# Square roots in batches of four chunks, paired exponentials and a new order of all queues, in a gated recurrence with a gated linear unit on one Trainium2 core

## The chip, the core and the metric

The kernel runs on one core of a Trainium2 chip. The core has a matrix engine (PE), three engines that work on whole tiles (DVE, ACT and POOL), a queue engine (SP) that here issues the transfers, and 16 DMA engines that carry them between the chip's main memory and the core's own memory, SBUF. Matrix results land in PSUM, eight banks of 128 partitions by 2 KB. Each engine works through its own list of instructions in order and waits at semaphores for the others. The metric is the device time of one execution in microseconds (us); less is better. Beside the timed runs there is one execution recorded by the hardware profiler; its span runs from the first to the last instruction.

## What is computed

The input is a batch of 4 sequences of 6336 steps with 256 channels, taken as 25344 rows. A gated linear recurrence runs along each sequence, and its result goes through a gated linear unit whose gate is a causal convolution of five taps:

```python
sig_r, sig_i = sigmoid(r_gate), sigmoid(i_gate)
a_t = np.exp(8.0 * sig_r * np.log(clip(sigmoid(a_param))))
x_gated = np.sqrt(np.maximum(1.0 - a_t * a_t, 1e-06)) * sig_i * x
for t in range(S):
    h = a_t[:, t] * h + x_gated[:, t]
    y[:, t] = h
...
gate = sigmoid(sum(conv_w[k] * shifted(y, k) for k in range(5)))
out = (gate * (y @ w_val)) @ w_out
```

So every element of the gates r and i and of x is read once, and every output is written once: about 78 MB in and 26 MB out.

## The kernel before

**Tiles.** The rows are cut into 51 windows, of 512 rows but for two of 256 at the start and one at the end, and the windows into 28 chunks (CHUNKS, line 16): the first three and the last two are small, the 23 between hold two windows, 1024 rows. Window w of a large chunk c is 2c-3 or 2c-2. Channels are handled in two halves of 128, called h.

**One chunk's way.** Loads of a window are `lr` (gate r), `li` (gate i) and `lx` (x), issued by SP. `ta` and `tb` (ACT, lines 296 and 299) take the hyperbolic tangent of r and i, from which the sigmoids follow. `tr` (PE, line 343) turns the tangent of r so that channels lie on partitions; `ex` (ACT, line 359) makes the decays a of it into `aring`. `sq` squares them into `ering` (POOL, line 367; `sa` is the same on ACT). `rt` (ACT, line 386) takes the square root over a whole batch of chunks in place. `nt` (PE, line 401) turns the roots back, and `xg` (DVE, line 408) multiplies them into `uring`, which holds the product of the input gate and x: `pp` and `up` on POOL (lines 306, 318), or, for some windows, `xp` on PE and `uv` on DVE (lines 323, 332). `xt` (PE, line 417) turns that product, and `sc` (DVE, line 439) is the recurrence itself, a scan for each half, into `yring`. For each window `cv` (PE, line 451) is the convolution, `tg` (ACT, line 458) the tangent for its sigmoid, `vl` (PE, line 466) the product with w_val, `gv` (DVE, line 471) the gating, `ou` (PE, line 481) the product with w_out, `cd` or `ca` the copy out of PSUM on DVE (line 489) or ACT (line 491), and `st` (SP, line 502) the store.

**What sets the order.** Everything stands in one string, ORDER, of words such as `tr.7.1@0,1` (operation, chunk or window, half, PSUM banks). A loop at the end emits them one by one, so that each engine's list is the string's words for that engine, in their order. [...]

**Tables.** `ta`, `tb`, `tg` and `ex` need one table of functions on ACT, `rt` another. The loop at the end keeps track and puts a table load (line 518) wherever the next word needs the other one. BATCHES (line 19) says which chunks share a root: there are ten, of three large chunks in the middle. `op_rt` emits one instruction for each stretch of the batch that is contiguous in `ering`, all at once.

**Rings.** The decays and the squares have room for 5120 columns each (NA, NE), five large chunks. A chunk's `ex` therefore overwrites the decays of the chunk five before, and has to wait until their scans are done; its `sq` overwrites squares whose roots `nt` must have read. The loads of r and of i have four window slots each, x four, the tangents of r six, of i four, the gate tile three (NTG), the output tile four.

**Groups.** GROUPS (line 32) says which chunks share one `tr` and `ex`: two neighbours in the middle, but 11, 12, 21 and 22 each alone.

ACT's list before, up to the third root and from the last but one:

```
ta.0 ta.1 ta.2 ex.0.1 ex.1.1 ex.1.0 ex.2.0 ex.0.0 ta.3 ta.4 tb.2 ex.2.1 tb.0 ex.3.1 tb.1 ex.3.0 ta.6 ta.5 tb.3
rt.0 rt.1 tb.4 ex.5.0 tg.0 tb.5 tg.1 ex.5.1 tg.2 ta.8 ta.7 tb.6 ex.7.1 ex.7.0 tb.7 tg.3 rt.2
...
rt.8 tg.41 tg.40 tb.25 ex.26.0 ca.39.0 tb.26 tg.42 ca.40.0 ex.26.1 sa.26.1 sa.26.0 ca.41.0 tg.43 tb.27 tg.44 ca.42.0
rt.9 tg.45 ca.44.0 ca.43.0 tg.46 tg.48 ca.45.0 ca.46.0 tg.47 ca.48.0 tg.49 ca.47.0 tg.50 ca.49.0 ca.50.0
```

Of the kernel before, what the change touches and what calls it, by code (L numbers as in the profile page):

```python
# [8 lines left out]
P = 128  # L9
CONV_K = 5  # L10
FP32 = mybir.dt.float32
# [7 lines left out]
BATCHES = [[0, 1, 2], [3, 4], [5, 6, 7], [8, 9, 10], [11, 12, 13], [14, 15, 16], [17, 18, 19], [20, 21, 22], [23, 24, 25],  # L19
    [26, 27]]  # L20
# [3 lines left out]
NU = 10  # L24
# [7 lines left out]
GROUPS = [[0], [1], [2], [3, 4], [5, 6], [7, 8], [9, 10], [11], [12], [13, 14], [15, 16], [17, 18], [19, 20], [21], [22],  # L32
# [3 lines left out]
s_ident s_small s_kt s_diag lr.0 ta.0 tr.0.1@0 lr.1 ta.1 lr.2 ta.2 ex.0.1 tr.1.1@1 ex.1.1 tr.1.0@2 tr.2.0@3 ex.1.0  # L36
ex.2.0 tr.0.0@0 tr.2.1@4 lr.3 lr.4 ex.0.0 sq.0.1 sq.0.0 ta.3 lr.5 lr.6 ta.4 sq.2.0 tr.3.1@0,1 li.2 lx.2 tb.2 ex.2.1
li.0 sq.1.0 s_wl.1 tb.0 lx.0 li.1 sq.1.1 ex.3.1 sq.3.1 sq.4.1 lr.7 tb.1 pp.1 tr.3.0@2,3 ex.3.0 sq.4.0 xp.0@4 uv.0 lr.9
lr.10 ta.6 xp.2@0,1 lr.8 sq.3.0 li.4 li.3 ta.5 tb.3 sq.2.1 s_wl.3 lx.1 lx.4 xp.4@2,3 lx.3 rt.0 uv.2 lx.6 li.6 s_wl.2
s_wl.0 lr.13 up.1 li.5 li.8 nt.0@0 xg.0 nt.2@1 nt.1@0 li.7 uv.4 xt.0@5,4 pp.3 up.3 lx.5 lx.7 lr.14 lr.12 rt.1 xg.1  # L40
xg.2 sc.0.1 sc.0.0 nt.3@6,7 xg.3 tb.4 li.10 lx.8 lr.11 li.9 xt.2@0,1 tr.5.0@2,3 xt.1@4,5 ex.5.0 cv.0@6,7 tg.0 sc.1.1
tb.5 li.12 sc.1.0 xt.3@5,4 sc.2.1 cv.1@6,7 tr.5.1@2,3 tg.1 ex.5.1 sc.2.0 cv.2@0,1 xp.7@6,7 sc.3.0 sc.3.1 s_wcast
vl.1@2,3 gv.1 pp.6 pp.5 vl.0@4,5 up.6 lx.10 up.5 pp.8 gv.0 nt.4@2,3 ou.0.0@4 ou.1.0@5 uv.7 tg.2 ta.8 cd.1.0 sq.6.1
lx.9 li.11 cd.0.0 st.1 st.0 ta.7 up.8 tb.6 tr.7.1@0,1 ex.7.1 xg.4 tr.7.0@6,7 ex.7.0 tb.7 lx.11 vl.2@4,5 gv.2 lr.16
lx.12 li.13 xt.4@2,3 sc.4.1 cv.3@0,1 sq.6.0 sq.5.0 sq.5.1 tg.3 vl.3@4,5 xp.9@6,7 sc.4.0 sq.7.1 sq.7.0 rt.2 lr.15 lr.18
gv.3 pp.10 sq.8.1 uv.9 vl.5@0,1 ou.3.0@4,5 ou.2.0@2,3 cd.3.0 cd.2.0 li.14 lr.17 st.3 lx.13 xp.11@6,7 cv.5@2,3 uv.11
tg.5 st.2 up.10 lx.14 li.15 li.16 pp.12 nt.5@6,7 xg.5 tb.8 li.17 up.12 lx.16 li.18 ta.10 gv.5 ta.9 lr.20 cv.6@4,5
# [502 lines left out]
```

## Time and profile before

| | |
|---|---|
| median of 3 timed runs | 294.39 us (293.57 to 295.06) |
| span of the profiled execution | 291.5 us |
| busy: ACT, DVE, PE, POOL | 275.0, 247.3, 243.8, 233.0 us |
| instructions: ACT, DVE, PE, POOL | 198, 206, 2509, 155 |
| moved by DMA | 104.75 MB, mean 359 GB/s |

The profiled execution has no time of its own beside its span; the timed runs take in what lies around the span. "Busy" counts an engine as working, not as waiting at a semaphore. Lines of groups give the source line, the engine, what is written from what with its shape, the number, the busy time, the mean of one in ns, and the idle time of the engine just before these instructions with what ended it ("<-"). Lines in order of time give the start, the duration, and the same names; instructions of one line that follow one another are merged ("x2").

### The profile page before, as it was taken

What the parts mean: (1) busy time and instruction counts of PE and PEld (TensorE: products, weight loads), DVE (VectorE), ACT (ScalarE), POOL (GpSimd) and SP (SyncE); (2) the same over time, 40 slices, a digit from 0 to 9 for tenths busy, and PEclk for the clock granted to TensorE, in tenths of its full rate; (3) what the DMA queues carried; (4) which work ended last, traced back from release to release, by engine and by line L of the source; (5) the groups of instructions that cost most, each with busy time, mean ns of one, the idle gap of its engine ahead of it and who ended that gap; (6) DMA issues with size and microseconds to landing.
All of it is one profiled execution on the core that took longest, in us unless ns stands there. A gap on an engine that the chain in (4) does not pass through costs nothing.

```text
span 291.5 us, 6283 instructions
## 1 busy us (share of the span) xinstructions
PE 243.8 (84%) x2509; PEld 167.6 (57%) x2509; DVE 247.3 (85%) x206; ACT 275.0 (94%) x198; POOL 233.0 (80%) x155
## 2 busy tenths in 40 slices
PE   2281798997986988989888988899889998999993
PEld 1141475455744766567656666657457765767662
DVE  2030589988999999999999999999999999999891
ACT  7799989999999999999999999999999999999563
POOL 1449789999899899999996599998998799976000
PEclk9996789999999999999999999999999999999999
DMA  7999999999999999999999999999999958983354
GB/s 243 356 409 388 386 408 413 338 419 414 408 417 398 388 393 400 386 347 415 412 398 384 409 410 371 411 339 386 408 414 421 413 211 322 338 329 128 147 217 181
DMA packets 29996, 104.75 MB, mean 359 GB/s; under 512 B 3335, under 2 KB 3854, under 8 KB 29966
## 3 DMA queue, kind: packets, MB, share of 16 engines
q1 hardware_dynamic: 29952, 104.35, 92.6%
q8 instruction: 19, 0.31, 0.4%
q14 instruction: 11, 0.09, 0.1%
q10 hardware_dynamic: 14, 0.01, 0.0%
HBM read 78.39 MB, written 25.95 MB: 358 GB/s over the span
## 4 chain that ended last, share of the span: by engine, by line
ACT 39%; PE 18%; DMA 17%; DVE 12%; issue 12%; SPq 1%; ACTq 0%; DVEq 0%
ACT tbring L299 9%; DMA iring<-in_i_gate_dram 8%; DMA rring<-in_r_gate_dram 8%; ACT ering L386 8%; ACT tgring L458 7%; ACT taring L296 6%; DVE yring L439 5%; PE banks L481 5%; PE banks L451 4%; ACT L518 4%; PE banks L466 3%; ACT aring L359 3%; PE banks L401 3%; DVE oring L489 2%; DVE tgring L471 2%
## 5 line engine op out<-in xcount | busy, mean ns | idle before, releaser
L367 POOL TENSOR_TENSOR ering<-aring 128x1024 f32<-128x1024 f32 (+2 forms) x54 | 91.9, 1723 | 21.4 <-ACT aring L359 21.4
L439 DVE TENSOR_TENSOR_SCAN yring<-aring,yring,banks 128x1024 bf16<-128x1024 f32 (+5 forms) x54 | 105.9, 1988 | 1.3 <-PE banks L417 1.2
L318 POOL TENSOR_TENSOR uring<-tbring,xring 128x1024 bf16<-128x1024 bf16 (+1 forms) x45 | 94.5, 2112 | 3.0 <-PE banks L481 1.3
L451 PE MATMUL banks<-yring,diag 64*64 64x512 bf16 (+7 forms) x1080 | 62.2, 361 | 3.0 <-DVE oring L489 1.7
L471 DVE SCALAR_TENSOR_TENSOR tgring<-tgring,banks 128x1024 bf16<-128x1024 bf16 (+1 forms) x51 | 59.1, 1179 | 5.3 <-PE banks L466 3.1
L466 PE MATMUL banks<-yring,wv 128*128 128x512 bf16 (+4 forms) x216 | 49.5, 361 | 8.7 <-ACT tgring L458 4.2
L359 ACT ACTIVATE aring<-banks,khf 128x2048 f32<-128x2048 bf16 (+3 forms) x38 | 54.5, 1485 | 1.1 <-PE banks L343 1.1
L458 ACT ACTIVATE tgring<-banks 128x1024 bf16<-128x1024 f32 (+1 forms) x51 | 50.5, 1014 | 5.1 <-PE banks L481 3.3
L481 PE MATMUL banks<-wo,tgring 128*128 128x256 bf16 x396 | 50.4, 274 | 5.2 <-DVE tgring L471 3.2
L306 POOL TENSOR_SCALAR tbring<-tbring 128x1024 bf16<-128x1024 bf16 (+1 forms) x45 | 45.8, 1030 | 8.3 <-ACT tbring L299 8.3
L481 PEld LDWEIGHTS <-tgring 128*128 128x128 bf16 x396 | 41.7, 114 | 14.8 <-DVE tgring L471 6.6
L296 ACT ACTIVATE taring<-rring 128x2048 bf16<-128x2048 f32 (+2 forms) x28 | 47.5, 1722 | 1.8 <-DMA rring<-in_r_gate_dram 1.8
L299 ACT ACTIVATE tbring<-iring 128x2048 bf16<-128x2048 f32 (+2 forms) x28 | 48.1, 1727 | 0.6 <-DMA iring<-in_i_gate_dram 0.6
L386 ACT ACTIVATE ering<-ering 128x2048 bf16<-128x2048 f32 (+3 forms) x13 | 44.5, 3454 | 0.1
L451 PEld LDWEIGHTS <-diag 64*64 64x64 bf16 x1080 | 29.0, 106 | 26.9 <-issue 11.4
L408 DVE TENSOR_TENSOR uring<-banks,uring 128x2048 bf16<-128x2048 bf16 (+2 forms) x28 | 30.3, 1092 | 14.7 <-PE banks L401 12.3
L489 DVE COPY oring<-banks 128x1024 f32<-128x1024 f32 (+1 forms) x35 | 40.6, 1185 | 0.8 <-PE banks L481 0.4
L343 PE MATMUL banks<-ident_b,taring 128*128 128x128 bf16 x396 | 30.2, 233 | 9.4 <-ACT taring L296 9.0
L466 PEld LDWEIGHTS <-wv 128*128 128x128 bf16 x216 | 19.7, 97 | 29.8 <-issue 14.4
L343 PEld LDWEIGHTS <-taring 128*128 128x128 bf16 x396 | 25.9, 105 | 16.1 <-ACT taring L296 11.5
L401 PE MATMUL banks<-ident,ering 128*128 128x128 f32 x198 | 29.3, 293 | 3.6 <-ACT ering L386 2.5
L401 PEld LDWEIGHTS banks<-ident,ering 128*128 128x128 f32 x198 | 26.3, 206 | 8.9 <-ACT ering L386 2.7
(37 smaller groups left out, 135.7 us busy)
## 6 DMA issues: line engine op xcount, KB each, us to landing
rring<-in_r_gate_dram SPq DMA_DIRECT2D x48, 512.0 KB, 7.5
iring<-in_i_gate_dram SPq DMA_DIRECT2D x48, 512.0 KB, 8.3
xring<-in_x_dram SPq DMA_DIRECT2D x48, 512.0 KB, 7.5
out_dram<-oring SPq DMA_DIRECT2D x48, 512.0 KB, 5.8
rring<-in_r_gate_dram SPq DMA_DIRECT2D x3, 256.0 KB, 3.0
iring<-in_i_gate_dram SPq DMA_DIRECT2D x3, 256.0 KB, 7.4
xring<-in_x_dram SPq DMA_DIRECT2D x3, 256.0 KB, 7.6
out_dram<-oring SPq DMA_DIRECT2D x3, 256.0 KB, 4.1
```

What stands on the lines that cost most here:

```text
L296: nc.scalar.activation(**tangent(c, taring, NTR, rring, NRI))
L299: nc.scalar.activation(**tangent(c, tbring, NTI, iring, NII))
L318: nc.gpsimd.tensor_tensor(out=u, in0=t1, in1=xt, op=ALU.mult)
L367: nc.gpsimd.tensor_tensor(out=e, in0=a, in1=a, op=ALU.mult)
L386: nc.scalar.activation(out=ering[:].bitcast(BF16)[:, 4 * o:4 * o + 2 * n], in_=ering[:, 2 * o:2 * o + 2 * n], func=ACT.Sqrt, scale=-0.25, ...
L401: nc.tensor.transpose(out=bank[:, k:k + P], in_=ering[:, e + q:e + wins[w] // 2:nq], identity=ident[:])
L439: nc.vector.tensor_tensor_scan(out=yring[:, h, col:col + o1 - o0], data0=aring[:, h, a_at[c] + o0:a_at[c] + o1], data1=xT[:, o0:o1], initi ...
L451: nc.tensor.matmul(out=gp[oh * 64:oh * 64 + 64, h, a:b], lhsT=diag[half * 64:half * 64 + 64, h, k, :], rhs=yring[half * 64:half * 64 + 64, ...
L458: nc.scalar.activation(out=tgring[:, w % NTG, :, 0:wins[w]], in_=live.pop(("gp", w))[:, :, 0:wins[w]], func=ACT.Tanh, scale=0.5)
L466: nc.tensor.matmul(out=val[:, m, a:b], lhsT=wv[:, hk, m * P:(m + 1) * P], rhs=yring[:, hk, col:col + b - a], start=(hk == 0), stop=(hk == ...
L471: nc.vector.scalar_tensor_tensor(out=tgring[:, w % NTG, :, 0:wins[w]], in0=tgring[:, w % NTG, :, 0:wins[w]], scalar=1.0, in1=live.pop(("va ...
L481: nc.tensor.matmul(out=ops[:, j * D:(j + 1) * D], lhsT=gv[:, hk, j:wins[w]:J], rhs=wo[:, hk, :], start=(hk == 0), stop=(hk == H - 1))
```

## The change

Batches of the root become four large chunks in the middle and the last three chunks at the end; chunks 11, 12 and 21, 22 become pairs for the exponentials. The root's pieces become separate words (`rt.2.0`, `rt.2.1`), and so do the two halves of `xt`, each with one bank. The whole of ORDER is replaced: the order of every engine's list and of SP's transfers, the PSUM banks, the windows whose input product goes through PSUM (0, 1, 2, 8, 9, 18 in place of 0, 2, 4, 7, 9, 11), and the engine of the output copies (20 on ACT and 31 on DVE in place of 16 and 35). Of chunk 26 one half is squared on ACT in place of two. Ring sizes, shapes, loads and stores are the same.

```diff
-BATCHES = [[0, 1, 2], [3, 4], [5, 6, 7], [8, 9, 10], [11, 12, 13], [14, 15, 16], [17, 18, 19], [20, 21, 22], [23, 24, 25],
-    [26, 27]]
+BATCHES = [[0, 1, 2], [3, 4], [5, 6, 7, 8], [9, 10, 11, 12], [13, 14, 15, 16], [17, 18, 19, 20], [21, 22, 23, 24], [25,
+    26, 27]]
...
-GROUPS = [[0], [1], [2], [3, 4], [5, 6], [7, 8], [9, 10], [11], [12], [13, 14], [15, 16], [17, 18], [19, 20], [21], [22],
+GROUPS = [[0], [1], [2], [3, 4], [5, 6], [7, 8], [9, 10], [11, 12], [13, 14], [15, 16], [17, 18], [19, 20], [21, 22],
     [23, 24], [25], [26], [27]]
...
-        def op_rt(b):
-            cs = BATCHES[b]
-            k = 0
+        def root_pieces(b):
+
+            cs, got, k = BATCHES[b], [], 0
             while k < len(cs):
                 m = k + 1
                 while m < len(cs) and e_at[cs[m]] == e_at[cs[m - 1]] + clen[cs[m - 1]]:
                     m += 1
...
+                got.append(cs[k:m])
                 k = m
+            return got
+
+        def op_rt(b, k):
+            cs = root_pieces(b)[k]
+            o = e_at[cs[0]]
+            n = e_at[cs[-1]] + clen[cs[-1]] - o
+            nc.scalar.activation(out=ering[:].bitcast(BF16)[:, 4 * o:4 * o + 2 * n],
+                                 in_=ering[:, 2 * o:2 * o + 2 * n], func=ACT.Sqrt, scale=-0.25, bias=0.25)
+            for c in cs:
+                live["n", c] = H * o + e_at[c] - o
...
-        def op_xt(c, *at):
-            for h in range(H):
-                bank = banks[:, at[h]]
+        def op_xt(c, h, at):
+            bank = banks[:, at]
```

With the columns of the ring, the roots after are pieces of 2048, 4096 | 4096 and 4096 | 6144 and 2048 | 8192 | 8192 | 2048 and 6144 | 3584 columns; bars part visits to the root's table. ACT's list after, in the same two stretches and around the next roots:

```
ta.0 ta.2 ta.1 ex.0.1 ex.2.0 ex.1.1 ex.2.1 tb.0 ex.1.0 ex.0.0 ta.3 ta.4 tb.2 ex.3.1 ex.3.0 tb.3 tb.1 rt.0.0 rt.1.0
ta.5 ta.6 tg.0 tb.4 tg.1 ex.5.1 ex.5.0 tb.5 tg.2 ta.7 ta.8 tg.3 ex.7.0 tb.6 tg.4 ex.7.1 tb.7 tg.5 rt.2.0 rt.2.1
ta.10 ta.9 tg.6 tb.8 tb.9 ex.9.1 ex.9.0 tg.7 ta.12 tg.9 ta.11 tg.8 ex.11.0 tb.10 ex.11.1 tb.11 tg.11 tg.10 ta.14
tg.12 rt.3.0 rt.3.1 tb.12 tg.13 ta.13 tg.14 tb.13 ex.13.1 ex.13.0 tg.15 ta.15 ca.13.0 ta.16 tg.16 ex.15.0 tg.17
tb.15 ex.15.1 tg.18 tb.14 ta.17 tg.20 tg.19 rt.4.0 tg.21 tb.16 ta.18 tg.22 tb.17 ex.17.1
...
ca.38.0 tb.26 tb.25 tg.41 ca.40.0 ca.39.0 ex.26.0 sa.26.1 tb.27 tg.42 tg.43
rt.7.0 tg.45 tg.44 ca.43.0 ca.45.0 ca.44.0 tg.46 tg.47 ca.46.0 tg.48 tg.49 ca.47.0 ca.48.0 tg.50 ca.49.0 ca.50.0
```

DVE's list after, from the products of batch 5 to 8 to those of the next, and its last words:

```
xg.5 xg.6 sc.5.1 sc.5.0 xg.7 sc.6.1 gv.6 sc.7.1 sc.6.0 cd.6.0 gv.7 sc.7.0 gv.8 gv.9 cd.7.0 xg.8 cd.8.0 sc.8.1 sc.8.0
cd.9.0 gv.11 gv.12 gv.10 cd.11.0 uv.18 cd.12.0 cd.10.0 xg.9
...
xg.25 gv.45 gv.44 sc.25.1 sc.25.0 xg.26 xg.27 gv.46 sc.26.1 sc.26.0 gv.47 sc.27.1 gv.48 sc.27.0 gv.49 gv.50
```

## The prediction

> **What bounds the kernel now.** I first read the page's head and the busy time of each engine, then the stages.
>
> ```profile
> span 291.5 us, 6283 instructions
> ...
> PE 243.8 (84%) x2509; PEld 167.6 (57%) x2509; DVE 247.3 (85%) x206; ACT 275.0 (94%) x198; POOL 233.0 (80%) x155
> ```
>
> ACT is busiest, but 94% is an average over a start, a middle and an end. Next, the busy time in five stretches (the columns are length, then PE, PEld, DVE, ACT, POOL, granted clock, DMA share, GB/s):
>
> ```profile
> 0.00:36.00 36.00, 16.36 (x79) 10.38 (x80) 7.79 (x18) 31.76 (x28) 20.01 (x25) 0.89 0.96 356
> 36.00:60.00 24.00, 21.54 (x214) 14.20 (x213) 21.62 (x19) 22.90 (x16) 21.82 (x14) 0.96 1.01 388
> 60.00:255.00 195.00, 174.23 (x1892) 122.17 (x1894) 189.46 (x146) 194.62 (x129) 180.94 (x110) 1.00 0.99 386
> 255.00:275.00 20.00, 19.98 (x216) 13.26 (x205) 20.00 (x15) 16.64 (x18) 10.21 (x7) 1.00 0.59 222
> 275.00:291.50 16.50, 11.69 (x123) 7.55 (x120) 8.44 (x11) 9.12 (x10) 0.00 (x0) 0.98 0.44 176
> ```
>
> From 60 to 255 us ACT is idle for 0.4 us of 195: it paces the middle, and a microsecond of ACT work taken out there is a microsecond, if nobody else takes its place. The nearest are DVE (5.5 us idle of 195) and the DMA (share 0.99). In the last stretches ACT has holes and PE and DVE are full until 275: the tail is a chain of handovers. What ACT and the load queue waited for says on which side the DMA stands:
>
> ```profile
> ACT taring L296 <- DMA rring<-in_r_gate_dram: 1.8, 2, 1.5
> ...
> ACT tbring L299 <- DMA iring<-in_i_gate_dram: 0.6, 1, 0.6
> ```
>
> ```profile
> SPq L278 <- ACT taring L296: 20.8, 12, 4.7
> ```
>
> ACT waited 2.4 us for data in all, and the loads waited 20.8 us for ACT to read an old slot: the loads follow ACT, not the other way round.
>
> **The change, part by part.** All prices on ACT come from its groups by shape (busy, mean ns of one):
>
> ```profile
> L458 ACT ACTIVATE tgring<-banks 128x1024 bf16<-128x1024 f32 x48 | 48.8, 1040 | 5.1 <-PE banks L481 3.3 <-PE banks L451 1.7
> L299 ACT ACTIVATE tbring<-iring 128x2048 bf16<-128x2048 f32 x23 | 44.1, 1929 | 0.6 <-DMA iring<-in_i_gate_dram 0.6
> L296 ACT ACTIVATE taring<-rring 128x2048 bf16<-128x2048 f32 x23 | 43.7, 1921 | 1.8 <-DMA rring<-in_r_gate_dram 1.8
> L359 ACT ACTIVATE aring<-banks,khf 128x2048 f32<-128x2048 bf16 x18 | 36.8, 2085 | 1.1 <-PE banks L343 1.1
> L518 ACT ACT_TABLE_LOAD x18 | 23.1, 1283 | 0.3
> L386 ACT ACTIVATE ering<-ering 128x6144 bf16<-128x6144 f32 x4 | 21.3, 5333 | 0.0
> L491 ACT COPY oring<-banks 128x1024 f32<-128x1024 f32 x15 | 15.0, 1021 | 1.5 <-PE banks L481 1.0 <-ACT oring L491 0.5
> ...
> L359 ACT ACTIVATE aring<-banks,khf 128x1024 f32<-128x1024 bf16 x10 | 11.9, 1230 | 0.0
> ...
> L375 ACT ACTIVATE ering<-aring 128x512 f32<-128x512 f32 x2 | 1.2, 624 | 0.0
> ```
>
> *Tables.* In the order before, the ten roots make nine visits to the root's table (the first two are neighbours): 18 loads. After, eight batches in seven visits (pieces of one batch, and the first two batches, have no table user between them): 14. Four loads by 1.283 = -5.13 us. Whether a switch costs more than its load is seen in ACT's order of time around one:
>
> ```profile
> 82.00 1.03 ACT L458 ACTIVATE tgring<-banks 128x1024 bf16<-128x1024 f32 x1
> 83.05 1.28 ACT L518 ACT_TABLE_LOAD   x1
> 84.34 5.33 ACT L386 ACTIVATE ering<-ering 128x6144 bf16<-128x6144 f32 x1
> ```
>
> The load starts 0.02 us after the tanh and the root 0.01 us after the load, so 1.28 is the whole price. The Trainium skill (ScalarE: Activation LUTs, What ACT_TABLE_LOAD costs) adds a drain of about 1.38 us to each load, some 2.66 us a switch; by it the four would save an estimated 10.6 us, but these rows leave no room for a drain, and I keep theirs.
>
> *Exponentials.* Chunks 11, 12 and 21, 22 become pairs: eight instructions of 1.230 become four of 2.085, -1.50 us. *Square.* One of the two halves of chunk 26 on ACT goes to POOL, -0.62 us; POOL has 9.8 us free between 255 and 275, and the half stands there ahead of the last squares, before the last root: uncovered it would cost about what it saves. *Root pieces.* The same elements in 11 instructions instead of 13. From 5.333 us for 6144 and 1.49 for 1536 (row below) an element costs 0.83 ns and a start some 0.2 us: -0.4 us. *Copies.* 20 of the 51 output copies are on ACT instead of 16: +4.08 us there. *Tanh of the gate.* One more (window 44) stands behind the last root: -1.04 us ahead of it. Sum on ACT up to the end of the last root: -5.13 - 1.50 - 0.62 - 0.40 + 4.08 - 1.04 = **-4.6 us**.
>
> *DVE.* Four copies and one of eleven PSUM products fewer:
>
> ```profile
> L439 DVE TENSOR_TENSOR_SCAN yring<-aring,yring,banks 128x1024 bf16<-128x1024 f32 x40 | 92.3, 2334 | 0.1
> L471 DVE SCALAR_TENSOR_TENSOR tgring<-tgring,banks 128x1024 bf16<-128x1024 bf16 x48 | 57.0, 1210 | 3.5 <-PE banks L466 1.4 <-PE banks L417 0.7 <-ACT tgring L458 0.7
> L489 DVE COPY oring<-banks 128x1024 f32<-128x1024 f32 x33 | 39.3, 1215 | 0.7 <-PE banks L481 0.4 <-issue 0.2
> L408 DVE TENSOR_TENSOR uring<-banks,uring 128x2048 bf16<-128x2048 bf16 x23 | 27.8, 1215 | 3.9 <-issue 2.3 <-PE banks L401 1.4
> L332 DVE SCALAR_TENSOR_TENSOR uring<-tbring,banks 128x512 bf16<-128x512 bf16 x11 | 7.7, 735 | 14.2 <-PE banks L323 14.1
> ```
>
> That is 4 x 1.215 + 0.74 = 5.6 us, so the second engine in line is relieved by at least as much as the first. That is why I believe the ACT saving is not simply caught by DVE.
>
> *Transposes by half* (op_xt) are the same 198 matmuls in 56 steps instead of 28; a second half may now stand behind another PE step of 1.2 us, which the 2.33 us scan of the first half hides. Without that cover it is 1.2 us a chunk. *Windows through PSUM* (0, 1, 2, 8, 9, 18 for 0, 2, 4, 7, 9, 11) leave half a window more, some 1.6 us, on POOL, which is idle 14 us of the middle.
>
> *The start.* Before, two tanhs of the next batch stand ahead of the first root:
>
> ```profile
> 21.40 3.71 ACT L296 ACTIVATE taring<-rring 128x2048 bf16<-128x2048 f32 x2 [0.35 <-DMA rring<-in_r_gate_dram]
> ...
> 28.89 5.42 ACT L386 ACTIVATE ering<-ering 128x2048 bf16<-128x2048 f32 x2
> ...
> 38.60 2.06 ACT L359 ACTIVATE aring<-banks,khf 128x2048 f32<-128x2048 bf16 x1 [1.07 <-PE banks L343]
> ```
>
> After, ta.5 and ta.6 come behind it, so the root starts some 4.6 us earlier (3.71 and the waits of 0.35 and 0.6). For ACT the work is only moved; what it gains are waits: between 0 (each returns elsewhere) and 2.0 (0.35 + 0.6 + 1.07 all go); I take -1.0. DVE, idle 28 us of the first 36, starts scanning some 4 us earlier.
>
> *The queues.* All 153 loads and 51 stores stay, in another order on SP; every engine's order and the banks change. A load that is late stops ACT. The price is between 0 and, if each of the five later roots (batches of four) cost a wait as long as the longest of the start (1.07), 5.4 us. The row of 60 to 255 us (0.4 in all) is nearest, but it belongs to an order that fits these durations; I take +1.0.
>
> *The tail.* The root's end sets it. Before, on ACT and DVE:
>
> ```profile
> 265.45 1.49 ACT L386 ACTIVATE ering<-ering 128x1536 bf16<-128x1536 f32 x1
> ...
> 287.57 0.59 ACT L491 COPY oring<-banks 128x512 f32<-128x512 f32 x1 [0.88 <-PE banks L481]
> ```
>
> ```profile
> 267.60 4.58 DVE L439 TENSOR_TENSOR_SCAN yring<-aring,yring,banks 128x1024 bf16<-128x1024 f32 x2
> ...
> 277.65 2.44 DVE L439 TENSOR_TENSOR_SCAN yring<-aring,yring,banks 128x512 bf16<-128x512 f32 x2
> ```
>
> The last root ends at 266.9, the span 24.6 us later. The scans of chunk 25 started 0.7 us behind it, because chunk 25 belonged to the batch before. After, it is in the last batch: its transposes (1.2, eight matmuls), its product (1.2) and the gates of windows 45 and 44 (2.4) come first, so the scans start 4.9 us behind the root, +4.2. Between them and the scans of chunk 26 lay 10.05 us with four gates and two small products; now one gate and the same products, 4.6 + 1.1 + 1.2 = 6.9, -3.2. One gate (window 48) moves behind the scans of 26: +1.2. Together +2.2, bounds 0 (all in PE's shadow) and 4.2; I take **+2.0**.
>
> *Sum* against the profiled span: 291.5 - 4.6 - 1.0 + 1.0 + 2.0 = **288.9 us**. The median of the runs shown, 294.39, lies 2.9 above the profiled span; I keep that: **291.8 us**.
>
> *DVE as a check.* 247.3 - 5.6 = 241.7 busy; idle before 44.2 (28.2 + 2.4 + 5.5 + 0 + 8.1), less 4 at the start: 281.9. So DVE may wait 7 us more than before and still not be the bound.
>
> **The rivals.** *The scan loop closes too late (slower).* The ring of decays holds five large chunks, and a batch now takes four of them: the exponentials of chunks 11 and 12 overwrite 6 and 7, so they wait on ACT, with tanhs, roots and hence loads queued behind, for scans of chunk 7, which need the root of 5 to 8. From the end of that root's first piece DVE needs 1.2 (transposes) + 3 x 1.215 + 6 x 2.334 + 2 x 1.21 + 1.215 = 22.5 us; ACT meanwhile does the second piece (3.6), a table (1.3), four ta (7.7), two tb (3.9), two pair exponentials (4.2) and four tg (4.2) = 24.9. The slack is 2.4 us. Handovers eat it:
>
> ```profile
> 65.89 1.22 DVE L408 TENSOR_TENSOR uring<-banks,uring 128x2048 bf16<-128x2048 bf16 x1 [1.37 <-issue]
> 67.42 1.22 DVE L471 SCALAR_TENSOR_TENSOR tgring<-tgring,banks 128x1024 bf16<-128x1024 bf16 x1 [0.31 <-ACT tgring L458]
> 68.82 2.36 DVE L408 TENSOR_TENSOR uring<-banks,uring 128x2048 bf16<-128x2048 bf16 x2 [0.18 <-PE banks L401]
> ```
>
> Here they were 1.9 us at one root. If they are twice that, ACT stands 1.4 us in each of five batches: 7 us in place of my 1.0, span 294.9, **297.8 us**. It decides from 0.7 us a batch (3.6 / 5). Against it: behind the single root of 13 to 16 the first pair (17, 18) needs 1.2 + 3 x 1.2 + 2.33 = 7.1 us of DVE against a table, two tg and three tanhs of inputs on ACT, 9.1, so 2 us are left there too, and DVE has 7 us to give over the kernel.
>
> *The DMA is the bound (no change).* For it: a share of 0.99 for 195 us. Then ACT only waits where it computed, and the time stays at **294.4**. Against it: 2.4 us of waits, and a stretch that moved 421:
>
> ```profile
> 60.00:64.00 4.00, 4.00 (x32) 2.50 (x34) 4.00 (x6) 4.00 (x2) 4.00 (x3) 1.00 1.04 421
> ```
>
> That is 9% over the 386 of the middle, where 1% is asked for. The Trainium skill (DMA: Bandwidth & Descriptors, Where 436 GB/s comes from) lets the HBM side bind at about 358 GB/s, by which the kernel could not get faster; these rows lie above it for 195 us, so I give it no more than this.
>
> *More than forecast.* No new waits and the tail as before: 291.5 - 4.6 - 1.0 = 285.9, **288.8 us**.
>
> **How the numbers follow.** Forecast 0.50 (290.3 to 293.6), scan loop 0.25, DMA 0.12, more 0.13. A measurement of this kernel tells about 0.5% (1.5 us) from no change. Faster: 0.42 + 0.13 + 0.02 = 0.57; the same: 0.08 + 0.07 + 0.03 = 0.18; slower: 0.22 + 0.03 = 0.25. The range reaches from the good rival, 288.5, to the scan loop, 298.5.
>
> **What would show it.** Right: 14 table loads; ACT idle under 2 us from 60 us to its last tanh of inputs; the last root ending near 262.3; DVE idle of some 10 us in the middle. Wrong: ACT idle before ering or aring lines L359 released by DVE scans (the loop); ACT idle released by loads of r or i (the DMA); a tail over 28.8 us from the last root to the end. Should ACT stand more than 3.6 us longer than before between 36 us and the last root, the gain is gone whatever the cause.

## The result, and the profile after

The changed kernel takes 292.88 us in the median of 20 runs (290.90 to 295.00), the kernel before, run beside it, 294.27 us (292.64 to 296.56). The ratio is 0.9946, with a 95% interval of 0.9927 to 0.9965: 0.5% faster, 1.4 us by the medians, where 2.6 were forecast. The head of the page of the changed kernel:

```profile
span 291.6 us, 6228 instructions
...
PE 244.7 (84%) x2482; PEld 168.5 (58%) x2507; DVE 243.5 (83%) x201; ACT 272.4 (93%) x191; POOL 235.2 (81%) x156
```

The profiled span is 0.1 us longer than that of before. That isn't the result: every one of the 20 runs lists a span that lies 1.7 to 1.8 us under its time, so the profiled execution after stands for 293.4 us, half a microsecond above its median, and the one before (291.5) for about 293.3, 1 us below its median. Two single profiles differ here by more than the change brings. They show where time went, stretch by stretch, and not how much in all.

The groups of ACT of the changed kernel, by shape (busy us, mean ns of one, idle just before them):

```profile
L360 ACT ACTIVATE aring<-banks,khf 128x2048 f32<-128x2048 bf16 x22 | 45.1, 2071 | 0.7 <-POOL ering L368 0.3 <-PE banks L344 0.2
...
L496 ACT COPY oring<-banks 128x1024 f32<-128x1024 f32 x19 | 19.3, 1030 | 4.8 <-PE banks L486 4.8
L523 ACT ACT_TABLE_LOAD x14 | 18.0, 1283 | 0.2
L393 ACT ACTIVATE ering<-ering 128x8192 bf16<-128x8192 f32 x2 | 14.1, 7035 | 0.0
```

There are 14 table loads at the same 1.283 us, four pair exponentials more, and a root of 8192 columns takes 7.035 us. Now the two kernels in three stretches: start to the first root behind the neighbours (before: that of chunks 5 to 7, after: of 5 to 8), from there to the last root, from the last root to the end. The columns are as in the prediction, the fifth is ACT. First the kernel before:

```profile
0.00:59.62 59.62, 37.60 (x289) 24.35 (x289) 29.04 (x36) 54.29 (x42) 41.45 (x38) 0.91 0.98 369
59.62:265.45 205.83, 184.97 (x1997) 129.46 (x1996) 200.29 (x155) 205.10 (x141) 190.02 (x117) 1.00 0.98 381
265.45:291.50 26.05, 21.24 (x225) 13.75 (x224) 17.99 (x17) 15.65 (x16) 1.51 (x2) 0.98 0.41 165
```

And the changed kernel, in the same three stretches and then from 60 to 255 us:

```profile
0.00:62.78 62.78, 42.45 (x339) 26.98 (x342) 31.90 (x39) 56.35 (x44) 43.70 (x38) 0.92 0.97 366
62.78:261.26 198.48, 177.07 (x1896) 124.48 (x1915) 188.97 (x143) 197.45 (x131) 184.15 (x116) 1.00 0.98 383
261.26:291.60 30.34, 25.19 (x251) 16.99 (x252) 22.58 (x21) 18.59 (x17) 7.29 (x4) 0.99 0.48 191
...
60.00:255.00 195.00, 173.69 (x1830) 122.67 (x1847) 185.64 (x142) 194.05 (x126) 181.17 (x111) 1.00 0.98 387
```

The start is 3.2 us longer (2.1 of it work of ACT, 1.1 idle time), the middle 7.35 us shorter (7.65 less work, 0.3 more idle time), and from the last root to the end it is 4.3 us longer. Of the start, 0.7 us lies ahead of all that was changed: in this profile ACT's first tanh of r starts at 5.44 us, in the one of before at 4.75. ACT still paces the middle: idle for 1.0 us of 198.5. DVE is now idle for 9.4 us of the 195. What ACT waited for in the changed kernel, in the whole execution, longest first (us in total, times, longest; the opening instructions' own rows are left out):

```profile
ACT oring L496 <- PE banks L486: 5.8, 7, 1.5
ACT tgring L463 <- PE banks L456: 4.1, 6, 1.8
ACT taring L297 <- DMA rring<-in_r_gate_dram: 1.9, 1, 1.9
...
ACT aring L360 <- POOL ering L368: 0.3, 1, 0.3
```

The copies of L496 wait behind the last root. No wait on DVE's scans is among them, and one load was late, in the start.

How the tail was lengthened shows on DVE, in order of time (start, duration; in brackets the idle time and what ended it):

```profile
266.11 1.23 DVE L414 TENSOR_TENSOR uring<-banks,uring 128x2048 bf16<-128x2048 bf16 x1 [0.35 <-PE banks L407]
267.25 2.34 DVE L476 SCALAR_TENSOR_TENSOR tgring<-tgring,banks 128x1024 bf16<-128x1024 bf16 x2
269.51 4.58 DVE L444 TENSOR_TENSOR_SCAN yring<-aring,yring,banks 128x1024 bf16<-128x1024 f32 x2
...
276.20 1.27 DVE L444 TENSOR_TENSOR_SCAN yring<-aring,yring,banks 128x512 bf16<-128x512 f32 x1
```

The last root ran from 261.26 for 3.19 us and ended at 264.45. The scans of chunk 25 start 5.06 us behind that, the scans of 26 another 6.69 us later, and the span ends 15.4 us after those. Before, the same three distances were 0.66, 10.05 and 13.85 us. Together the end of the root is 27.15 us ahead of the end of the span, where it was 24.55.

### The profile page after: what moved, and what is told of

Same layout as the page of the kernel before. It is cut to its first block, busy times and chain, and to the rows that moved or that the text cites. A ratio compares the mean times of both kernels' runs of the same rounds, so it can differ in the third digit from the quotient of the medians.

```text
span 291.6 us, 6228 instructions
## 1 busy us (share of the span) xinstructions
PE 244.7 (84%) x2482; PEld 168.5 (58%) x2507; DVE 243.5 (83%) x201; ACT 272.4 (93%) x191; POOL 235.2 (81%) x156
## 5 line engine op out<-in xcount | busy, mean ns | idle before, releaser
L456 PE MATMUL banks<-yring,diag 64*64 64x512 bf16 (+7 forms) x1080 | 63.2, 365 | 1.4 <-DVE tgring L476 0.4
L360 ACT ACTIVATE aring<-banks,khf 128x2048 f32<-128x2048 bf16 (+3 forms) x34 | 53.4, 1610 | 0.7 <-POOL ering L368 0.3
L471 PE MATMUL banks<-yring,wv 128*128 128x512 bf16 (+7 forms) x191 | 48.4, 359 | 4.9 <-ACT aring L360 1.6
L456 PEld LDWEIGHTS <-diag 64*64 64x64 bf16 x1080 | 30.3, 107 | 25.2 <-issue 9.7
L393 ACT ACTIVATE ering<-ering 128x2048 bf16<-128x2048 f32 (+4 forms) x11 | 44.1, 4042 | 0.1
L494 DVE COPY oring<-banks 128x1024 f32<-128x1024 f32 (+1 forms) x31 | 36.3, 1182 | 3.6 <-PE banks L486 3.5
L422 PE MATMUL banks<-ident,uring 128*128 128x128 f32 x198 | 30.8, 283 | 7.8 <-DVE uring L414 4.4
L422 PEld LDWEIGHTS banks<-ident,uring 128*128 128x128 f32 x198 | 22.0, 142 | 16.3 <-DVE uring L414 7.6
```

Of the source, the lines that this page charges most:

```text
L360: nc.scalar.activation(out=dst, in_=src, func=ACT.Exp, scale=khf[:, h:h + 1], bias=khf[:, h:h + 1])
L422: nc.tensor.transpose(out=bank[:, o + q:o + wins[w] // 2:nq], in_=uring[:, (w + 1) % NU, q, h * P:(h + 1) * P, :].rearrange("p d two -> p ...
L456: nc.tensor.matmul(out=gp[oh * 64:oh * 64 + 64, h, a:b], lhsT=diag[half * 64:half * 64 + 64, h, k, :], rhs=yring[half * 64:half * 64 + 64, ...
L471: nc.tensor.matmul(out=val[:, m, a:b], lhsT=wv[:, hk, m * P:(m + 1) * P], rhs=yring[:, hk, col:col + b - a], start=(hk == 0), stop=(hk == ...
```

## The experiments

Times are medians; each ratio is to the kernel before, run beside the kernel in question, with its 95% interval. The kernel before took 294.27 us beside the changed kernel, 294.35 beside b1 and the three with an a, 294.23 beside those with a c, and 294.09 beside those with a d.

| kernel | us | ratio | interval |
|---|---|---|---|
| changed kernel | 292.88 | 0.9946 | 0.9927 to 0.9965 |
| changed kernel, again (d2) | 292.67 | 0.9954 | 0.9925 to 0.9984 |
| before, four loads fewer (b1) | 293.40 | 0.9958 | 0.9927 to 0.9988 |
| before, four copies on ACT (c1) | 298.81 | 1.0149 | 1.0105 to 1.0192 |
| before, both (c2) | 297.33 | 1.0093 | 1.0061 to 1.0125 |
| after, four loads more (a2) | 299.76 | 1.0159 | 1.0113 to 1.0205 |
| after, four copies back on DVE (a3) | 295.80 | 1.0047 | 1.0021 to 1.0073 |
| after, tanhs ahead of the first root (d4) | 303.04 | 1.0312 | 1.0280 to 1.0344 |
| after, PE kept busy (a4) | 292.34 | 0.9929 | 0.9894 to 0.9965 |
| after, PE kept busy, again (d1) | 291.55 | 0.9915 | 0.9886 to 0.9944 |
| after, short convolution at the end (c3) | 291.59 | 0.9917 | 0.9884 to 0.9949 |
| after, last root split (c4) | 293.31 | 0.9954 | 0.9926 to 0.9982 |
| after, two copies left out (d3) | 292.56 | 0.9949 | 0.9925 to 0.9972 |

**Is a microsecond of ACT a microsecond? The tables.** In the kernel before, batches 3 and 6 use a function that is in the table already loaded, so that four loads fall away; the roots of these two batches are left out:

```diff
-                                 in_=ering[:, 2 * o:2 * o + 2 * n], func=ACT.Sqrt, scale=-0.25, bias=0.25)
+                                 in_=ering[:, 2 * o:2 * o + 2 * n], func=ACT.Square if b in (3, 6) else ACT.Sqrt,
+                                 scale=-0.25, bias=0.25)
...
-if table.get(name, have) != have:
+if word not in ("rt.3", "rt.6") and table.get(name, have) != have:
```

> The kernel before, with batches 3 and 6 computed as squares in the table of the exponentials, so that four table loads fall away (18 to 14) and nothing else moves; these batches' results are left out. If ACT paces the middle, four loads of 1.28 us are worth all or most of 5.1 us: time 289.2 to 290.5 against 294.3, ratio 0.983 to 0.987. If the transfers or DVE pace it beside ACT, the loads are worth less than half: ratio 0.991 to 1.000.

It gained about 1.2 us (0.4 to 2.1 by the interval) for 5.1 us of ACT's work, some 24%. The two profiles show the same: from the root of chunks 5 to 7 to the last root it is 204.65 us, where it was 205.83. The busy times of this kernel from 60 to 255 us:

```profile
60.00:255.00 195.00, 175.69 (x1896) 122.42 (x1898) 190.45 (x147) 190.58 (x126) 181.37 (x111) 1.00 0.99 386
```

Before, ACT stood 0.4 us here; now it stands 4.4. One of the new waits, in the list of what ACT waited for:

```profile
ACT ering L386 <- POOL ering L367: 2.2, 2, 1.1
```

Two roots, those without a load ahead of them, wait for POOL's squares, 1.1 us each; until then the load of 1.28 us had covered that. Two more waits of ACT there, 1.1 us for POOL's products and 0.9 for PE's convolution, are new as well. So POOL and PE came little earlier than before, and ACT now waits at the places where it would have come earlier.

The other way about, two more visits' worth of loads in the changed kernel (two pairs of loads, with no root between them):

```diff
-ta.16
+sw ta.16
...
-ta.20
+sw ta.20
...
+        def op_sw():
+            nc.scalar.preload_act_table_set("sqrt_and_others")
+            nc.scalar.preload_act_table_set("exp_and_others")
```

> The changed kernel with two more visits to the root's table (four loads, 5.1 us of ACT) in the middle, ahead of ta.16 and of ta.20. If ACT paces: 5.1 us more than the changed kernel, 298.0, ratio to the kernel before about 1.012. If ACT has room beside another bound: 293 to 295, ratio 0.997 to 1.003.

It cost 6.9 us against the changed kernel's 292.88 (5.3 to 7.9 by the runs of the two) for 5.1 us of ACT: not less than the work, unlike the saving. Its busy times from 60 to 255 us:

```profile
60.00:255.00 195.00, 170.58 (x1783) 119.64 (x1782) 177.56 (x137) 191.39 (x122) 173.96 (x106) 0.97 0.97 374
```

There is more in it than the loads. Behind them PE stands 2.7 and 3.0 us for tanhs of ACT, and its granted clock, 1.00 in the changed kernel here, falls to 0.50 from 130 to 135 us and to 0.74 from 175 to 180. ACT stands 3.6 us in all, where it stood 1.0; its longest new wait, 1.6 us, is for PE at 140 us. So what exceeds the 5.1 us need not be the price of the loads themselves.

**The copies.** In the kernel before, four output copies go from DVE to ACT:

```diff
-cd.13.0
+ca.13.0
...
-cd.21.0
+ca.21.0
...
-cd.28.0
+ca.28.0
...
-cd.29.0
+ca.29.0
```

> The kernel before, with the copies of windows 13, 21, 28 and 29 on ACT in place of DVE (ACT 4.1 us more, DVE 4.9 less), tables untouched. If ACT and DVE are both full in the middle (idle 0.4 and 5.5 us of 195): 2 to 4 us slower, 296 to 298. If DVE alone paces the kernel before: 2 to 4 us faster, 290 to 292.

And both edits in one kernel:

```diff
+                                 in_=ering[:, 2 * o:2 * o + 2 * n], func=ACT.Square if b in (3, 6) else ACT.Sqrt,
...
+ca.13.0
...
+ca.21.0
...
+ca.28.0
...
+ca.29.0
```

> The kernel before with both: batches 3 and 6 as squares without their four table loads (their results are left out) and the four copies of windows 13, 21, 28 and 29 on ACT. If the saving on ACT only counts when DVE is relieved too: 3 to 5 us faster, 289.5 to 291.5, more than the tables alone (1.0 us) and the copies alone together. If something behind both (PE, the end) holds: 292.5 to 294.

The copies alone cost 4.4 us (3.1 to 5.6 by the interval); four of them take 4.1 on ACT. The profile of the kernel with the copies alone, from 60 to 255 us:

```profile
60.00:255.00 195.00, 170.19 (x1852) 118.94 (x1851) 182.09 (x140) 194.61 (x129) 177.24 (x108) 1.00 0.98 378
```

ACT still stands only 0.4 us, DVE now 12.9: work added to ACT is paid in full here, and DVE's relief is worth nothing by itself. Both edits together were expected to gain 3 to 5 us, since each engine then has less to do than before; they cost 2.7 (1.0093), close to the sum of the two alone (-1.2 + 4.4), and the roots wait for POOL's squares as in the first. So these two pieces of the change don't make its gain by themselves: in the old order they lose together. In the changed kernel, where all five engines' lists are laid out again around them, the middle is 7.35 us shorter for 7.65 us less of ACT's work. Which part of the new order brings that is not shown; the paired exponentials, for one, were not run alone.

The reverse, with the four copies of the changed kernel given back to DVE:

```diff
-ca.13.0
+cd.13.0
...
-ca.20.0
+cd.20.0
...
-ca.21.0
+cd.21.0
...
-ca.28.0
+cd.28.0
```

> The changed kernel with the copies of windows 13, 20, 21 and 28 on DVE again (ACT 4.1 us less, DVE 4.9 more). If ACT alone paces and DVE has some 7 us to give: 2 to 4 us faster than the changed kernel, 289 to 291. If the scans, and so DVE with PE, close the loop as tightly as ACT: 0 to 3 us slower than it, 293 to 296.

It takes 2.9 us more than the changed kernel, with 4 us less work on ACT. Its busy times from 60 to 255 us, and then one row of what ACT waited for and two of what PE waited for:

```profile
60.00:255.00 195.00, 171.96 (x1826) 120.39 (x1825) 187.05 (x145) 187.91 (x119) 178.93 (x109) 1.00 0.99 385
```

```profile
ACT aring L361 <- DVE yring L445: 2.3, 2, 1.9
```

```profile
PE banks L345 <- DVE oring L495: 2.2, 2, 1.9
...
PE banks L457 <- DVE oring L495: 1.6, 1, 1.6
```

ACT now stands 7.1 us of the 195. Two exponentials wait 2.3 us for DVE's scans, a wait that the changed kernel doesn't have. This is the scan loop of the prediction's first rival: it is there, and 4.9 us more on DVE, spread over four places, are enough to close it too late. But that is the smaller part. PE waits for PSUM banks that the copies given back to DVE hold, in two rows that the changed kernel lacks, and behind them gates and an exponential on ACT wait 4.0 us for PE between 60 and 255 us, where it was 0.2. The longest, 2.2 us, is the gate at 170.59: the convolution that it needs had waited 1.6 us for the copy of window 21.

**The start.** The two tanhs of the next batch go back ahead of the first root, as they stood before the change, and nothing else moves:

```diff
-s_wl.1 uv.1 rt.0.0 li.8
+s_wl.1 uv.1 ta.5 ta.6 rt.0.0 li.8
...
-xt.2.0@7 ta.5 xt.0.0@0
+xt.2.0@7 xt.0.0@0
...
-s_wcast ta.6 xg.3
+s_wcast xg.3
```

> The changed kernel with ta.5 and ta.6 ahead of the first root again, as in the kernel before. If moving them behind it gained what was forecast (1.0 us) or more, because they fill ACT while DVE and PE make the first scans: 1 to 4 us slower than the changed kernel. If the start hangs on transfers and the order of these two is indifferent: within 0.5 us.

It takes 10.4 us more than the changed kernel run beside it; 1 to 4 were expected. ACT in order of time in this kernel:

```profile
27.84 1.91 ACT L298 ACTIVATE taring<-rring 128x2048 bf16<-128x2048 f32 x1 [4.06 <-DMA rring<-in_r_gate_dram]
31.77 1.91 ACT L298 ACTIVATE taring<-rring 128x2048 bf16<-128x2048 f32 x1 [2.02 <-DMA rring<-in_r_gate_dram]
33.69 1.28 ACT L524 ACT_TABLE_LOAD   x1
34.99 5.42 ACT L394 ACTIVATE ering<-ering 128x2048 bf16<-128x2048 f32 x2
...
46.79 0.60 ACT L464 ACTIVATE tgring<-banks 128x512 bf16<-128x512 f32 x1 [5.09 <-PE banks L457]
```

And the same part of the changed kernel:

```profile
24.77 1.28 ACT L523 ACT_TABLE_LOAD   x1
26.07 5.42 ACT L393 ACTIVATE ering<-ering 128x2048 bf16<-128x2048 f32 x2
31.50 1.28 ACT L523 ACT_TABLE_LOAD   x1
32.80 3.71 ACT L297 ACTIVATE taring<-rring 128x2048 bf16<-128x2048 f32 x2
37.66 0.60 ACT L463 ACTIVATE tgring<-banks 128x512 bf16<-128x512 f32 x1 [1.15 <-PE banks L456]
```

From the end of the first roots to the first gate it is 6.2 us in the changed kernel and 6.4 in the other: that is how long PE, DVE and PE again take to turn roots into a window. In the changed kernel the two tanhs fill this hole. Ahead of the root they wait 6.1 us for their loads, whose places in SP's list were not moved back with them, and then leave the hole empty. The root starts 8.9 us later (9.7 against the changed kernel's second profile) and nothing is won back: a step is worth the hole that it fills, and its loads belong to its place. The 10.4 us are the price of both together; the two tanhs moved with their loads were not run.

**What the runs differ by.** The changed kernel was run once more (no edit):

> The changed kernel as it is: 292.5 to 293.3, and a profile whose stretch from the root of batch 5 to 8 to the last root is 198.4 to 198.6 us, with the difference to its first profile (291.6) made ahead of that stretch.

Its median is 292.67, 0.2 us from the first. Lengths in us of the three stretches in the profiles with the changed order, from the same kind of windows as above:

| profile | start to root of 5 to 8 | to the last root | last root to end | span |
|---|---|---|---|---|
| changed | 62.78 | 198.48 | 30.34 | 291.6 |
| again (d2) | 61.55 | 198.46 | 30.39 | 290.4 |
| PE kept busy (a4) | 60.44 | 198.42 | 30.64 | 289.5 |
| PE kept busy (d1) | 60.76 | 198.55 | 30.39 | 289.7 |
| last root split (c4) | 63.92 | 198.45 | 30.43 | 292.8 |
| tanhs first (d4) | 72.13 | 198.47 | 30.30 | 300.9 |
| copies left out (d3) | 61.29 | 199.37 | 30.24 | 290.9 |
| short convolution (c3) | 63.74 | 199.50 | 29.76 | 293.0 |

But for two, the middles repeat to within 0.13 us, whatever came before them, and the tails, but for the one with an edit there (c3), to within 0.4. ACT paces the middle so strictly that a late start is neither made up nor made worse. The two middles that are 0.9 and 1.0 us longer hold one late load of r each: a tanh waits 0.81 us for it at 123.69 (d3) and 0.92 at 126.27 (c3). So the transfers do stop ACT in the middle of some executions. Otherwise the spans differ mostly by what happened ahead of the root of chunks 5 to 8.

One thing that differs there is PE's clock. From 24 to 28 us and again from 34 to 36, in windows of 2 us (PE's busy time is the second number, the granted clock the seventh):

```profile
22.00:24.00 2.00, 0.17 (x1) 0.17 (x2) 0.29 (x1) 1.68 (x1) 2.00 (x3) 1.00 1.02 408
24.00:26.00 2.00, 2.00 (x4) 0.91 (x5) 0.00 (x0) 1.98 (x3) 2.00 (x2) 0.67 1.03 412
26.00:28.00 2.00, 2.00 (x3) 0.42 (x2) 0.00 (x0) 1.99 (x3) 2.00 (x2) 0.50 1.00 399
...
34.00:36.00 2.00, 2.00 (x12) 2.00 (x10) 1.44 (x2) 2.00 (x2) 2.00 (x4) 0.50 1.03 410
```

PE stands while it waits for a piece of x, and the work that follows runs at half the clock. The second fall stands behind shorter waits, of 1.3, 0.8 and 0.8 us from 28.8 us on. The change did not bring this: in the kernel before, the clock is 0.50 from 26 to 30 us, in and behind a wait of PE of 7.1. So 96 small matmuls were put into its idle time in five places of the start; their results go into a bank that is free there and are not used:

```diff
+        def op_wm(n):
+            for k in range(n):
+                nc.tensor.matmul(out=banks[:, 1, 128 * (k % 4):128 * (k % 4) + 128], lhsT=ident_b[:], rhs=ident_b[:],
+                                 start=True, stop=True)
...
-xp.0@3
+xp.0@3 wm.40
...
-nt.1@7
+nt.1@7 wm.20
...
-xt.0.1@2
+xt.0.1@2 wm.12
...
-xt.1.0@3
+xt.1.0@3 wm.12
...
-xt.2.1@6
+xt.2.1@6 wm.12
```

> The changed kernel with 96 small matmuls more, in five places between 20 and 36 us where PE waits, into a PSUM bank that nobody uses then. In its 20 runs the span rises as the mean granted clock falls (289.1 at 0.994, 293.2 at 0.975). If the clock that PE is granted in the first 40 us delays the start: mean clock 0.99 or more, 1 to 2 us faster than the changed kernel, and a narrower spread. If the lower clock is only a sign of late transfers: no change or up to 1 us slower.

> The changed kernel with the 96 small matmuls at the start once more, beside the changed kernel itself on the same chip. Their first profiles had the root of batch 5 to 8 at 60.4 us against 62.8 to 63.9, and no wait of ACT for the first convolution. If the PE clock of the start costs time: 1 to 2 us faster than the changed kernel of this call. If not: within 0.5 us of it.

The first stretch of the second of these profiles, and PE's products of x in the first of them:

```profile
0.00:60.76 60.76, 43.89 (x436) 30.45 (x439) 31.95 (x39) 56.24 (x45) 43.72 (x38) 1.00 0.97 374
```

```profile
22.88 2.84 PE L325 MATMUL banks<-xring,ident 128*128 128x512 f32 x6 [0.29 <-DMA xring<-in_x_dram]
```

In the first profile of the changed kernel PE came to the same six matmuls later, 0.7 us of it from the opening, and they took longer:

```profile
23.83 4.54 PE L324 MATMUL banks<-xring,ident 128*128 128x512 f32 x6 [2.40 <-DMA xring<-in_x_dram]
```

With PE kept busy the clock is 1.00 throughout, and ACT's idle time in the start is 4.2 and 4.5 us against 6.4 and 5.2 in the two profiles of the changed kernel (0.7 of the 6.4 being the opening). The medians are 0.5 us under the first measurement of the changed kernel and 1.1 us under the second, which ran beside d1. Compared directly, the runs of that second pair differ by 1.3 us in the mean (0.5 to 2.0 with 95%), those of the first by 0.3 (0.8 slower to 1.3 faster): the gain is shown where the two ran side by side, and not by the first pair. These two are the fastest kernels found among those that leave nothing out, 0.7 to 0.85% under the kernel before. The kernel before was not run with such matmuls. The clock isn't all of the spread: with it at 0.995 or above in all nine runs of the first, their spans still went from 288.8 to 293.0. What else moves the start stays open.

**The tail.** Three attempts to shorten it, each by relieving one of those that hand over there. PE: the convolution of windows 45 to 50 is one tap, four are left out.

```diff
+            taps = range(CONV_K) if w < 45 else [CONV_K - 1]
             for a, b, col in pieces(w):
-                for k in range(CONV_K):
+                for k in taps:
```

> The changed kernel with one tap in place of five in the convolutions of the last six windows, 45 to 50 (four taps of them are left out): some 5 us of PE less behind the last root. If PE paces the end (the chain of waits is PE alone from 237 us): 3 to 5 us faster than the changed kernel, 288 to 290. If the end is the chain root, scan, gate, store: 0 to 1 us faster, 292 to 293.

ACT: the last root in two pieces, chunk 25 first.

```diff
-                while m < len(cs) and e_at[cs[m]] == e_at[cs[m - 1]] + clen[cs[m - 1]]:
+                while m < len(cs) and cs[m] != 26 and e_at[cs[m]] == e_at[cs[m - 1]] + clen[cs[m - 1]]:
...
-rt.7.0
+rt.7.0 rt.7.1
```

> The changed kernel with its last root in two pieces, chunk 25 first and 26 and 27 behind it, in one visit to the table: chunk 25's roots are ready 1.3 us earlier, ACT pays 0.2 us. If the tail hangs on that root: 1.0 to 1.3 us faster than the changed kernel, 291.6 to 291.9. If PE paces the end: within 0.3 us of it, 292.6 to 293.2.

DVE: the output copies of windows 41 and 42 are left out.

```diff
-vl.43@4,5 cd.41.0 up.47
+vl.43@4,5 up.47
...
-cv.45@6,7 cd.42.0 up.49
+cv.45@6,7 up.49
```

> The changed kernel without the output copies of windows 41 and 42 (their outputs are left out), which stand on DVE just ahead of the product of chunk 25. If DVE's list carries the end (5 us less of PE there gave only 0.6 us of a shorter tail, an earlier root nothing): 1.5 to 2.4 us faster than the changed kernel, tail of 25 to 25.6 us behind the last root in place of 27.1. If the end hangs on the last root through PE: within 0.5 us, tail 27.

By the profiles, neither of the last two shortened the tail (30.43 and 30.24 against 30.34 and 30.39 us), and the short convolution, with 4 us less on PE, by half a microsecond (29.76). Its median of 291.59 is the lower by more than that, but its interval takes in the changed kernel's ratio. Why the tail didn't start earlier can be read around the transposes of chunk 25 (L407 in the changed kernel and with the short convolution, L408 in the other two). PE in the changed kernel:

```profile
263.57 1.27 PE L456 MATMUL banks<-yring,diag 64*64 64x512 bf16 x20
264.77 1.23 PE L407 MATMUL banks<-ident,ering 128*128 128x128 f32 x8
```

The root ends at 264.45, PE's convolution at 264.84, and the gate on DVE that frees the two banks runs 1.21 us from 263.41, to 264.62: three conditions within 0.4 us. With the short convolution PE was early, and waited for that gate, which ran until 266.60:

```profile
266.74 1.20 PE L407 MATMUL banks<-ident,ering 128*128 128x128 f32 x8 [0.79 <-DVE tgring L477]
```

With the root split, the two pieces took 3.29 us from 262.37, and the first was ready some 1.4 us ahead of the second (an estimate, from the 1.9 us of a root of 2048 columns, three in 5.7 us). PE and then DVE show there:

```profile
264.68 1.27 PE L457 MATMUL banks<-yring,diag 64*64 64x512 bf16 x20
265.89 1.23 PE L408 MATMUL banks<-ident,ering 128*128 128x128 f32 x8
```

```profile
264.52 1.21 DVE L477 SCALAR_TENSOR_TENSOR tgring<-tgring,banks 128x1024 bf16<-128x1024 bf16 x1
...
267.22 1.23 DVE L415 TENSOR_TENSOR uring<-banks,uring 128x2048 bf16<-128x2048 bf16 x1 [0.36 <-PE banks L408]
```

PE and DVE come as late as ever. Without the two copies DVE was early, and stood while PE finished its convolution at 264.24 and then the transposes:

```profile
262.27 1.22 DVE L477 SCALAR_TENSOR_TENSOR tgring<-tgring,banks 128x1024 bf16<-128x1024 bf16 x1 [0.52 <-PE banks L472]
265.50 1.22 DVE L415 TENSOR_TENSOR uring<-banks,uring 128x2048 bf16<-128x2048 bf16 x1 [2.01 <-PE banks L408]
```

In all four kernels the transposes start 3.5 us behind the start of the last root. With PE relieved the gate on DVE holds them, and with the gate or the root relieved PE's convolution does; that the root would hold them with both of these out of the way is not shown. Relieving all three at once was not tried, nor is it known what the rest of the tail would do then: from 266.11 to 284.35 us DVE of the changed kernel goes on with 0.8 us of idle time, and may be the next to bind.

## Why the prediction came out as it did

The direction holds, and so does the mechanism for ACT's work, the middle and the tail. One step, the start, came out the other way, and that the time lies so near the forecast is in part luck: two errors cancel, as the offset below shows. Against the pair of profiles, step by step (what was forecast, what the windows and groups show):

| step | forecast | measured |
|---|---|---|
| ACT's work up to the end of the last root | -4.6 | -3.9 |
| start, ACT's idle time | -1.0 | +1.1 |
| new waits from the start to the last root | +1.0 | +0.3 |
| tail, from the root's end | +2.0 | +2.6 |
| sum, in the profiled spans | -2.6 | +0.1 |
| time above the profiled span of before | 2.9 | 1.8 |
| difference of the medians | -2.6 | -1.4 |

- **ACT's work.** Busy up to the end of the last root was 54.29 + 205.10 + 1.49 = 260.9 us and is 56.35 + 197.45 + 3.19 = 257.0. The tables gave the 5.1 us and the loads lasted 1.283, with no drain; the root pieces gave 0.4 and the square half a microsecond. Mis-sized were the exponentials: 1.5 forecast, and the busy time of all of them together fell from 54.5 to 53.4 us, by 1.1. The working multiplied mean durations, and successive instructions of ACT overlap at their ends, as in ACT's order of time in the changed kernel:

```profile
256.58 0.73 ACT L376 ACTIVATE ering<-aring 128x512 f32<-128x512 f32 x1
257.10 0.73 ACT L300 ACTIVATE tbring<-iring 128x512 bf16<-128x512 f32 x1
```

  The square lasts 0.73 us and the next instruction starts 0.52 us after it did. An instruction less saves its spacing, not its duration. The copies, forecast at 4.08, cost 4.3.
- **The start.** This is the step that failed: -1.0 was taken, between 0 and -2.0, and +1.1 came out. The root does start earlier, but by 2.8 us (26.07 against 28.89) and not by 4.6, and the two tanhs do fill a hole, as the experiment with them put back shows. In this profile 0.7 of the 1.1 us is the opening, ahead of all that was changed. Another 0.4 is the tanh of chunk 4, which waits 1.89 us for its load of r where it waited 1.46. Its row before, in the changed kernel, and in the changed kernel's second profile:

```profile
12.59 1.91 ACT L296 ACTIVATE taring<-rring 128x2048 bf16<-128x2048 f32 x1 [1.46 <-DMA rring<-in_r_gate_dram]
```

```profile
14.96 1.91 ACT L297 ACTIVATE taring<-rring 128x2048 bf16<-128x2048 f32 x1 [1.89 <-DMA rring<-in_r_gate_dram]
```

```profile
14.60 1.91 ACT L297 ACTIVATE taring<-rring 128x2048 bf16<-128x2048 f32 x1 [2.20 <-DMA rring<-in_r_gate_dram]
```

  The three waits that were to go (0.35, 0.56 and 1.07) are gone, but four others stand in their place: 0.18, 0.32, 0.30 and, at the first gate in the rows above, 1.15 for PE's convolution. The second profile of the changed kernel, with an opening like that of before, has 5.2 us of idle time in the start (61.55 - 56.37) against the 5.3 of before. There the new waits are 1.0 in place of 2.0, the microsecond that was forecast, but the load of r took 0.7 of it back (2.20 us against 1.46). The forecast had a term for late loads behind the later roots and none for this one.
- **The waits in the middle.** They were to be between 0 and 5.4, taken as 1.0, and are 0.3 more than before (1.03 against 0.73). The argument that DVE is relieved by more than ACT was right where it was checked: DVE idle 9.4 us of the 195, where some 10 were named.
- **The tail.** The three terms were +4.2, -3.2 and +1.2, and are 5.06 - 0.66 = +4.4, 6.69 - 10.05 = -3.4 and +1.55. The mechanism is the one described, chunk 25 in the last batch; rounding 2.2 down to 2.0 went the wrong way.
- **The offset.** The prediction kept the 2.9 us between the median and the profiled span as a constant. It is 1.8 in nearly every run; the remaining 1.1 belongs to that one profile, whose span was short. It is luck that two errors partly cancel: the span came out at 288.9, 2.1 us under the median span of the changed kernel's runs (291.05), and the offset was 1.1 us too long, which leaves 291.8 against 292.9.
- **The rivals.** The scan loop did not decide: no exponential waits for a scan. It was near, though. With 4.9 us back on DVE it appears, with 2.3 us on ACT, so its slack is less than those 4.9. The DMA as the bound is refuted: ACT has one wait for a load in 291.6 us, in the start, and the middle became 7.35 us shorter at 387 GB/s from 60 to 255 us. In two other profiles a load in the middle came 0.8 and 0.9 us late, so it is not far off. The better rival (no new waits, the tail as before) failed by the tail and by the start. The range that the forecast gave for both sides, 288.5 to 298.5, reaches 0.3 and 0.7 us beyond its rivals' own times of 288.8 and 297.8; nothing hangs on that.
- **The signs that were named.** 14 loads, ACT idle 0.95 us from 60 to 255, DVE some 10, the tail 27.1 us and not over 28.8: as named. The last root ended at 264.45, not 262.3, 2.1 us late: 0.7 from the work, 1.4 from idle time.
- **The premise.** "A microsecond of ACT is a microsecond" was argued from 0.4 us of idle time in 195, and it is half true. Work added costs at least its length, in both orders (4.4 us for four copies of 1.02, 6.9 for 5.1 of loads, the latter with a fall of PE's clock in it). Work taken out of the order before does not give it: 5.1 us gave 1.2. In the change 7.65 us less work made the middle 7.35 us shorter; that the new order of the other lists is the reason is argued from this and not shown.

## What to carry to other kernels

In this kernel the engine that is never idle charged in full for what was added to it, but paid for what was taken away only so far as the others arrived earlier too. In an order fitted to all engines, look at who is second at each handover, and count a saving as an upper bound until the order is made again. Before costing a step by its profile, learn how far one profiled execution lies from the median (here 1 us, as much as the gain), and cost instructions by the spacing of their starts, not by their durations. Where several engines arrive at one handover within half a microsecond, relieving one of them gains nothing, and that says nothing against the handover.

## What the hardware did that was not expected

The clock that PE was granted fell to half in the start of a kernel that is otherwise busy, behind a wait of 2.4 us for a load, and six matmuls that take 2.84 us at full clock took 4.54. With four table loads more it fell in the middle too, behind waits of 2.7 and 3.0 us. Cheap matmuls in the gaps kept it at 1.00 through the first 60 us.

The Trainium skill (TensorE: Matmul & The Clock Gate, Part 1: The HAM clock gate) says that the array's clock halves after an idle window of about 3.4 us, and that the window runs free of what the kernel does. The rows agree with the half clock (0.50), but the waits that they show ahead of it in the changed order, up to 3.0 us, are shorter than that window. The same part of the Trainium skill puts the loss from warming up under 1% of a usual span. Here keeping PE busy was worth 1.1 us of 293 by the medians of the pair run side by side, under 1% too, but close to the 1.4 us of the change under study.
